# One DMA for a 128-row result tile in place of two of 64 rows, in a kernel of cosine attention and a two-layer product

## The chip, the cores and the metric

One core of a Trainium2 chip runs the whole kernel. The metric is the device time of one execution in microseconds, as the median of several runs. The profile is one more execution, recorded by the hardware profiler. Its span is some microseconds under the device time.

## What is computed

Attention with normalised q and k over 8 batches, 12 heads, 448 positions and 64 channels, then a two-layer product with a hard-swish between the layers, over 3584 tokens:

```python
q_n = q / (norm(q) + 1e-6);  k_n = k / (norm(k) + 1e-6)
attn = softmax(q_n @ k_n.T / tau)
x = (attn @ v)            # 3584 tokens x 768, tokens = batch x position
h = x @ w_in              # 768 -> 2048
g = h * clip(h + 3, 0, 6) / 6
out = g @ w_out           # 2048 -> 768, float32
```

Only the store of `out` is touched here: 3584 rows of 768 float32, 11.0 MB.

## The kernel before

The program is laid out by hand: a plan gives the order of all steps, and each engine runs its own in that order. Heads are treated in pairs, 48 in all. SyncE issues nearly all transfers, on one queue: the loads of q and k (`raw`) and v (`vr`), the transposes by DMA that turn normalised q and k into `tT` and the attention's result into `xT`, and the stores of the result.

```python
def load_qk(j, *heads):            # 448 KB; a load runs two to three pairs ahead of its use
    ...
    nc.sync.dma_start(out=raw_of[j][:, g, :, :].rearrange("p g c d -> p g (c d)"), in_=f[:, g, :])

def load_v(d):                     # four DMAs of 128 KB
    ...
            nc.sync.dma_start(out=o, in_=f[:, :, 3 * half * D : (3 * half + 4) * D])

def crossbar(j):                   # normalised q or k -> tT
    ...
    nc.sync.dma_start_transpose(out=crossed(j)..., in_=nrm...)

def back_crossbar(i):              # attention's result -> xT
    ...
    nc.sync.dma_start_transpose(out=xT[b % 2]..., in_=on...)
```

Positions are read so that partition p of a head holds positions 7p to 7p + 6. Column c (0 to 6) of that grouping gives 64 positions, one in seven. A row tile of the second product holds the 64 positions of one column and then the 64 of another: two columns c and c + 1 of one batch, or, in the fourth tile of a pair of batches, column 6 of the batch before and column 0 of this one.

One unit of the second product is 16 matmuls for 128 rows and 384 columns. The result leaves PSUM through ScalarE and VectorE in turn into `o` (four buffers) and goes to memory from there:

```python
def mm2_unit(b, t, m, end=None):
    ...
    width = MH if end is None else MH // 2          # MH = 384
    cols = slice(m * MH + width * (end or 0), m * MH + width * (end or 0) + width)
    for fc in range(FCN):                           # 16
        ...
        nc.tensor.matmul(ps[:, 0:width], lhs, w_out_sb[:, fc, cols], start=..., stop=...)

    def store():
        o = sb.tile([128, MH], FP32, name="o", tag="o", bufs=4)
        if on_act:
            nc.scalar.copy(out=o[:, 0:width], in_=ps[:, 0:width])
        else:
            nc.vector.tensor_copy(out=o[:, 0:width], in_=ps[:, 0:width])
        unread[key] = 0
        for e in range(2):
            if t < 3:
                r = out[b * S : (b + 1) * S].rearrange("(p c) m -> c p m", c=7)[2 * t + e + b % 2]
            else:
                r = out[(b - 1 + e) * S : (b + e) * S].rearrange("(p c) m -> c p m", c=7)[6 * (1 - e)]
            eng = nc.scalar if end == 1 and e else nc.sync
            eng.dma_start(out=r[:, cols], in_=o[64 * e : 64 * e + 64, 0:width])
```

The very last unit is cut in two of 192 columns, so that its second half is short. There are 55 full units and two half ones: 57 units and 114 stores. A store of 64 rows goes to rows that lie 7 x 768 floats apart, 1536 bytes in each.

Of the kernel before, what the change touches and what calls it, by code (L numbers as in the profile page):

```python
# [61 lines left out]
def kernel(  # L62
# [10 lines left out]
    nc = tc.nc  # L73
    B, H, S, D = q.shape
    d_model, d_ff = moe_w_in.shape
# [194 lines left out]
    def bank_of(name, reads):  # L270

        bank = {"Y": Y, "Z": Z}[name] if name else next_bank()
        key = id(bank)
        assert not unread.get(key), name
        unread[key] = reads
        return bank, key
# [246 lines left out]
    def mm2_unit(b, t, m, end=None):  # L523
        assert not weights
        g = gT[(b // 2) % 2]
        ps, key = bank_of(None, 1)
        width = MH if end is None else MH // 2
        cols = slice(m * MH + width * (end or 0), m * MH + width * (end or 0) + width)
        for fc in range(FCN):
            c0 = (S + SR) * (b % 2) + 128 * t if t < 3 else SM  # L530
            lhs = g[:, fc, c0 : c0 + 128]
            nc.tensor.matmul(  # L532
                ps[:, 0:width],
                lhs,
                w_out_sb[:, fc, cols],
                start=(fc == 0),
                stop=(fc == FCN - 1),
# [6 lines that stand above are left out]
            else:  # L544
                nc.vector.tensor_copy(out=o[:, 0:width], in_=ps[:, 0:width])  # L545
            unread[key] = 0
            for e in range(2):
                if t < 3:
                    r = out[b * S : (b + 1) * S].rearrange("(p c) m -> c p m", c=7)[2 * t + e + b % 2]
                else:  # L550
                    r = out[(b - 1 + e) * S : (b + e) * S].rearrange("(p c) m -> c p m", c=7)[6 * (1 - e)]
                eng = nc.scalar if end == 1 and e else nc.sync
                eng.dma_start(out=r[:, cols], in_=o[64 * e : 64 * e + 64, 0:width])

        evac_n[0] += 1
        on_act = evac_n[0] % 2 == 1
        post["a" if on_act else "v"].append(store)

    def second(b):
# [205 lines left out]
```

## Time and profile before

| | |
|---|---|
| device time, median of 3 runs | 428.23 us (426.42 to 429.01) |
| span of the profiled execution | 422.8 us |
| TensorE busy | 411.1 us, 97% |
| ScalarE, VectorE, GpSimd busy | 64%, 52%, 43% |
| moved by DMA | 65.82 MB, 156 GB/s in the mean |
| stores of the result | 114, of 96 KB (four of 48 KB) |
| first and last store issued | 99.3 and 419.5 us |

How to read the page: its first part has the busy time of each engine; then come the span in 40 slices, the DMA queues with the share of 16 DMA engines that their packets took, the chain of work that ended last (followed back from the last instruction to what released each step), the costliest groups of instructions, and the DMA issues with the time from issue to landing. The letters SPq stand for SyncE's queue, where transfers are issued. A line such as "L553" is a line of the kernel; L553 is the store, L302 the transpose into `tT`, L480 that into `xT`, L174 the load of q and k, and L186 the load of v. In a timeline of SyncE, the first number of a row is when the issue began, the second how long the issuing took, and the last how many in a row.

### The profile page before, as it was taken

The page shows a single profiled execution, that of the slowest core. Times are in us where ns is not written, and L with a number is a line of the kernel's source. Part 1 is how long each engine was busy: PE and PEld are TensorE (multiplying, and loading weights), DVE is VectorE, ACT ScalarE, POOL GpSimd, SP SyncE. Part 2 cuts the span into 40 slices and gives each one's busy share as a digit, 9 for nine tenths or more (in the row PEclk, how much of TensorE's full clock was granted, in tenths as well). Part 3 has the DMA queues.
Part 4 walks back from the last instruction along what each step waited for, and adds up shares of the span by engine and source line. Part 5 has one row for each costly group of instructions (what it writes and reads, how often), then busy time and mean ns, then how long its engine had stood idle before and what let it go on. Part 6 is the DMA issues. An engine that isn't in the chain of part 4 may idle for free.

```text
span 422.8 us, 9251 instructions
## 1 busy us (share of the span) xinstructions
PE 411.1 (97%) x3574; PEld 243.2 (58%) x3575; DVE 217.7 (52%) x419; ACT 271.2 (64%) x593; POOL 181.1 (43%) x184
## 2 busy tenths in 40 slices
PE   6999999999997999999999999999999999999996
PEld 5556655556654555656555555555555555655564
DVE  7689777675443454465455454554554343214410
ACT  6899989977555765866756775676765675105400
POOL 5997787512235456365365464374472200000000
PEclk9999999999999999999999999999999999999999
DMA  8997999996879767676995856668666251330033
GB/s 287 307 244 201 243 194 226 220 194 145 210 170 203 174 175 138 167 194 127 179 193 136 183 156 156 158 154 188 164 160 95 63 75 33 70 75 19 2 75 76
DMA packets 94156, 65.82 MB, mean 156 GB/s; under 512 B 58656, under 2 KB 92576, under 8 KB 94112
## 3 DMA queue, kind: packets, MB, share of 16 engines
q1 hardware_dynamic: 90320, 58.89, 60.4%
q0 software_dynamic: 3712, 6.29, 8.7%
q8 instruction: 28, 0.46, 0.5%
q14 instruction: 16, 0.13, 0.1%
q10 hardware_dynamic: 80, 0.05, 0.0%
HBM read 47.19 MB, written 11.01 MB: 138 GB/s over the span
## 4 chain that ended last, share of the span: by engine, by line
PE 88%; ACT 4%; DMA 4%; SPq 2%; issue 1%; POOL 0%; DVE 0%; ACTq 0%; POOLq 0%
PE M L496 22%; PE M L532 22%; PE PV L433 11%; PE Y L496 6%; PE M L394 6%; PE Z L496 5%; PE Y L532 5%; PE Z L532 5%; ACT at L412 3%; DMA tT<-nrm 2%; PE Z L394 2%; DMA raw<-in_k_dram 1%; PE SC L394 1%; PE Y L394 1%; PE PV L603 1%; DMA vr<-in_v_dram 1%
## 5 line engine op out<-in xcount | busy, mean ns | idle before, releaser
L532 PEld LDWEIGHTS <-gT 128*128 128x128 bf16 x912 | 88.7, 98 | 58.6
L412 ACT ACTIVATE at<-M 128x448 bf16<-128x448 f32 x195 | 94.9, 568 | 30.5 <-PE M L394 25.3
L496 PEld LDWEIGHTS <-w_in_sb 128*128 128x128 bf16 x768 | 74.1, 98 | 67.1 <-issue 3.4
L532 PE MATMUL M<-w_out_sb,gT 128*128 128x384 bf16 (+1 forms) x640 | 106.0, 322 | 0.0
L496 PE MATMUL M<-xT,w_in_sb 128*128 128x448 bf16 x510 | 104.2, 352 | 0.0
L246 POOL TENSOR_TENSOR nrm<-raw,r 128x896 bf16<-128x896 f32 (+1 forms) x45 | 74.2, 1655 | 26.6 <-ACT r L234 22.9
L203 POOL TENSOR_TENSOR sq<-raw 128x896 f32<-128x896 f32 (+3 forms) x42 | 67.8, 1618 | 28.9 <-DMA raw<-in_k_dram 11.6
L511 DVE SCALAR_TENSOR_TENSOR gT<-u,M 128x448 bf16<-128x448 bf16 x85 | 52.5, 621 | 51.0 <-ACT u L505 49.8
L505 ACT ACTIVATE u<-M,half_bias 128x448 bf16<-128x448 f32 x85 | 55.1, 652 | 20.9 <-PE M L496 19.5
L433 PEld LDWEIGHTS <-at 128*128 128x128 bf16 x1344 | 53.3, 98 | 24.9 <-issue 17.7
L433 PE MATMUL PV<-vx,at 128*128 128x65 bf16 (+1 forms) x1344 | 63.9, 198 | 0.0
L215 DVE TENSOR_REDUCE n<-sq 128x14 f32<-128x896 f32 (+1 forms) x50 | 51.9, 1041 | 3.4 <-POOL nrm L246 2.0
L351 POOL COPY km<-tT 64x128 bf16<-64x128 bf16 x34 | 10.6, 312 | 94.1 <-DVE rc L448 33.7
L543 ACT COPY o<-M 128x384 f32<-128x384 f32 (+1 forms) x21 | 9.9, 471 | 40.9 <-PE M L532 40.9
L449 DVE TENSOR_TENSOR on<-PV,rc 128x512 bf16<-128x512 f32 x48 | 33.2, 692 | 3.5 <-DMA xT<-on 1.9
L545 DVE COPY o<-M 128x384 f32<-128x384 f32 (+1 forms) x19 | 10.4, 547 | 47.7 <-PE M L532 47.7
L394 PE MATMUL M<-tT,kz 64*128 64x448 bf16 (+1 forms) x172 | 33.4, 353 | 1.4 <-DMA tT<-nrm 0.5
L412 ACT ACTIVATE at<-Y 128x448 bf16<-128x448 f32 x48 | 27.4, 571 | 10.9 <-PE Z L394 10.9
L412 ACT ACTIVATE at<-Z 128x448 bf16<-128x448 f32 x51 | 29.0, 569 | 3.0 <-PE M L394 2.7
L496 PE MATMUL Y<-xT,w_in_sb 128*128 128x448 bf16 x138 | 29.9, 352 | 0.0
L448 DVE RECIPROCAL rc<-PV 128x8 f32<-128x8 f32 x48 | 9.9, 206 | 38.2 <-PE PV L433 34.9
L496 PE MATMUL Z<-xT,w_in_sb 128*128 128x448 bf16 x120 | 26.1, 352 | 2.0 <-DMA xT<-on 2.0
(78 smaller groups left out, 342.8 us busy)
## 6 DMA issues: line engine op xcount, KB each, us to landing
vr<-in_v_dram SPq DMA_DIRECT2D x96, 128.0 KB, 3.8
raw<-in_k_dram SPq DMA_DIRECT2D x24, 448.0 KB, 4.4
raw<-in_q_dram SPq DMA_DIRECT2D x24, 448.0 KB, 4.3
out_dram<-o SPq DMA_DIRECT2D x110, 96.0 KB, 2.2
w_in_sb<-in_moe_w_in_dram POOLq DMA_DIRECT2D x4, 768.0 KB, 12.1
w_out_sb<-in_moe_w_out_dram POOLq DMA_DIRECT2D x4, 768.0 KB, 11.2
xT<-on SPq DMA_TRANSPOSE x42, 3.8
tT<-nrm SPq DMA_TRANSPOSE x34, 2.9
```

The source lines that it names most:

```text
L203: engines[e].tensor_tensor(out=o, in0=i, in1=i, op=ALU.mult)
L215: nc.vector.tensor_reduce(out=n2s[d % 2][:, j % 2, c], in_=sq[:, :, :, :].rearrange("p g c d -> p (g c) d")[:, c, :], axis=AX.X, op=ALU.add,)
L246: engines[e].tensor_tensor(out=nrm[:, :, g, :].rearrange("p c g d -> p g c d"), in0=raw_of[j][:, g, :, :], in1=rs[d % 2][3][:, j % 2, :] . ...
L351: nc.gpsimd.tensor_copy(out=km[p, :, p], in_=z[p, 3, :, :])
L394: nc.tensor.matmul(o, ks, qt[rows], start=True, stop=True)
L412: nc.scalar.activation(out=o, in_=x, func=AF.Exp, scale=inv_tau)
L433: nc.tensor.matmul(o, at[:, n, q_cols(i // HP, j)], mv, start=(name == "A0" and j % 2 == 0), stop=last, skip_group_check=True,)
L449: nc.vector.tensor_tensor(out=on[:, :, :, :].rearrange("p (b j) h d -> p b (j h) d", b=2), in0=pv4[:, :, :, 0:D], in1=rc[:, :, :].to_broad ...
L496: nc.tensor.matmul(ps[:, 0:S], w_in_sb[:, cc, fc * 128 : (fc + 1) * 128], x[:, cc, 0:S], start=(cc == 0), stop=(cc == CC - 1),)
L505: nc.scalar.activation(out=u[:, :], in_=ps[:, 0:S], func=AF.Relu, bias=half_bias[:, :], scale=1.0 / 6.0)
L511: nc.vector.scalar_tensor_tensor(out=g[:, fc, c0 : c0 + S], in0=u[:, :], scalar=1.0, in1=ps[:, 0:S], op0=ALU.min, op1=ALU.mult,)
L532: nc.tensor.matmul(ps[:, 0:width], lhs, w_out_sb[:, fc, cols], start=(fc == 0), stop=(fc == FCN - 1),)
```

## The change

Each unit's tile is stored by one DMA from all 128 partitions. Its destination is written as a three-dimensional access pattern: 2 columns of the grouping, 64 rows of each, and the 384 (or 192) floats of a row. The distance between the two halves is one row, or, in the fourth tile, the 442 rows from column 6 of one batch to column 0 of the next. The last half store of the last unit goes out on SyncE as well, and no longer on ScalarE. It is meant to halve the number of stores, with their issuing and their waits.

```diff
-            for e in range(2):
-                if t < 3:
-                    r = out[b * S : (b + 1) * S].rearrange("(p c) m -> c p m", c=7)[2 * t + e + b % 2]
-                else:
-                    r = out[(b - 1 + e) * S : (b + e) * S].rearrange("(p c) m -> c p m", c=7)[6 * (1 - e)]
-                eng = nc.scalar if end == 1 and e else nc.sync
-                eng.dma_start(out=r[:, cols], in_=o[64 * e : 64 * e + 64, 0:width])
+            c = 2 * t + b % 2 if t < 3 else 6
+            row = b * S + c if t < 3 else (b - 1) * S + c
+            step = 1 if t < 3 else S - 6
+            r = bass.AP(
+                tensor=out.tensor,
+                offset=out.offset + row * d_model + cols.start,
+                ap=[[step * d_model, 2], [7 * d_model, 64], [1, width]],
+            )
+            nc.sync.dma_start(out=r, in_=o[:, 0:width])
```

## The prediction

> **What bounds the kernel now.** I read the page first: busy times, DMA queues, chain, DMA issues.
>
> ```profile
> span 422.8 us, 9251 instructions
> PE 411.1 (97%) x3574; PEld 243.2 (58%) x3575; DVE 217.7 (52%) x419; ACT 271.2 (64%) x593; POOL 181.1 (43%) x184
> ...
> q1 hardware_dynamic: 90320, 58.89, 60.4%
> ...
> PE 88%; ACT 4%; DMA 4%; SPq 2%; issue 1%; POOL 0%; DVE 0%; ACTq 0%; POOLq 0%
> ...
> out_dram<-o SPq DMA_DIRECT2D x110, 96.0 KB, 2.2
> ...
> xT<-on SPq DMA_TRANSPOSE x42, 3.8
> tT<-nrm SPq DMA_TRANSPOSE x34, 2.9
> ```
>
> TensorE is the bound: 88% of the chain that ended last, 97% busy. A store lands in 2.2 us and nothing on the chain waits for one. But q1, the queue of SyncE, carries everything together: loads of q, k and v, the transposes that feed TensorE (tT, xT), and the stores. Its packets already take 60.4% of all 16 DMA engines' time.
>
> Next, SyncE's timeline from 95 to 140 us, where stores begin, and the chain of waits over the same stretch.
>
> ```profile
> 99.33 3.67 SPq L553 DMA_DIRECT2D out_dram<-o  x4
> 103.10 1.27 SPq L302 DMA_TRANSPOSE tT<-nrm  x1
> ...
> 106.43 1.17 SPq L553 DMA_DIRECT2D out_dram<-o  x2
> 107.66 2.67 SPq L186 DMA_DIRECT2D vr<-in_v_dram  x4
> ...
> 126.46 1.25 SPq L302 DMA_TRANSPOSE tT<-nrm  x1
> 127.80 2.46 SPq L553 DMA_DIRECT2D out_dram<-o  x4
> 130.37 1.27 SPq L302 DMA_TRANSPOSE tT<-nrm  x1
> ```
>
> ```profile
> 109.72 3.11 DMA vr<-in_v_dram
> ...
> 126.46 3.53 DMA tT<-nrm
> ...
> 130.37 4.58 DMA tT<-nrm
> ```
>
> Transposes and v loads stand behind stores in one queue, and here the chain does wait for them. From 135 us on no DMA stands on it. Last, SyncE's timeline of the tail:
>
> ```profile
> 401.34 18.67 SPq L553 DMA_DIRECT2D out_dram<-o  x17
> ```
>
> Seven full units (two DMAs each) and two half ones (one of their DMAs from ScalarE) leave in 18.7 us: one full unit each 2.6 us, TensorE's pace.
>
> [...]
>
> 1. [...] the DMA is split over k engines, [...] Before: 64 partitions against 64 rows, k = 16. After: 128 partitions against a destination whose outermost dimension is 2, so k = 2. [...] The trace before agrees on the first half (the 64 packets of one store pass in 0.59 us, which one or two engines could not do); it holds no DMA with k below 16.
> 2. [...]
> 3. [...] Of the stores' 1536-byte packets, the shortest and about a fifth take 62 to 66 ns, the median 107 ns. [...]
>
> **The change part by part.**
>
> *Removed:* 57 of 114 store issues at 0.58 us (median of L553): 33 us of SyncE's queue time. SyncE's issuing stands for 2% of the chain, chiefly from 102 to 110 us, with three of the removed issues: at most 2 us gained. The evacuating copies wait for one DMA where they waited for two; no compute instruction is added or removed, and TensorE's order stays.
>
> *Changed:* the bytes, 11 MB, stay; their engines do not. At k = 2 each full store is 64 packets of 1536 bytes on engine 0 and 64 on engine 1. At 62 ns (packets of other sizes move in line: 1792 bytes 74 ns, 1024 bytes 46 ns, 256 bytes 18 ns, all medians of the packet records) that is **3.97 us on two engines**, against 4 packets on each of 16 per half-store. At 107 ns it would be 6.8 us.
>
> *Load of engines 0 and 1.* TensorE's stage of two pairs of heads lasts 16.0 us (by the timeline scores start at 223.5, 231.5 and 239.5 us, pair by pair). Issued in it: 2 raw loads of 16 packets for each engine (2 x 16 x 74 ns = 2.4 us), 4 v loads of 8 (1.5 us), 2 xT of 32 (1.2 us), 2 tT of 56 (2.0 us): 7.1 us. From 140 to 330 us the records hold 28 stores, 2.36 in 16 us: 9.4 us. Sum **16.5 us of work in 16.0 us**: these two engines become as full as TensorE, while the other 14 empty. Three stretches follow.
>
> *a. 99 to 135 us, replayed by hand on engine 0.* Two stores issued from 99.3 start about 1.3 us after issue and end at 108.5; two tT and one raw take it to 111.7, the next store to 115.7, the v loads to 117.2. With 0.9 us from last packet to semaphore v lands at 118, where it lands at 112.8: 5 us later. Ahead of the tT issued at 126.46 then lie three stores and 7.9 us of loads and xT: it ends at 138, 8 to 9 us late. Two stores lie between it and the tT of 130.37: that one lands near 147.6 against 134.95. **About 12.5 us lost.**
>
> *b. 135 to 340 us.* Overload 16.5/16.0 is 3%, some 6 us if the queue stays full. Added to it are waits. The tT of the query side is issued at 225.19 and its scores start at 231.54: 6.35 us, of which it uses 2.9. In that stage two stores are issued from 221.85, so 7.9 us of packets precede it, behind what is still queued: it lands about 2 us late. Stages with two such stores come four times (copies to o at 165, 221, 262 and 317 us), so four times 2 us. In the others one store of 4 us fits in the slack. As the overload and these waits partly cover one another, I choose **11 us**.
>
> *c. The tail.* The first store's packets start 1.3 us after 401.34, at 402.6. Then 7 x 3.97 + 2 x 64 x 34 ns (768-byte packets, shortest 34 ns) = 32.1 us on engines 0 and 1 without a gap (four buffers of o keep three stores queued): 434.7, landed at 435.2, against 421.7 before. **13.5 us lost**; TensorE finishes early and waits. The six units from 366 to 380 need 24 us and are through by 393, so they are not carried over.
>
> Sum: 12.5 + 11 + 13.5 = 37 us, less 1 for SyncE: 36 to 37. On the median of 428.2: **465 us**.
>
> **The rivals.**
>
> - *All 16 engines are still used* (the hardware splits on another dimension). [...] its packets fall from 107 towards 62 ns, and half the issues are gone. As stores aren't on the chain and the tail ends in one small store, this is worth 1 to 3 us: 425 to 428. For it: the trace has no DMA with small k. [...] I give it 5%.
> - *Two engines, but hidden.* Deep prefetch (seven raw buffers, two stages ahead) and four o buffers absorb the latency; only the tail shows: 428 + 13.5 = 441. For it: no DMA on the chain after 135 us. Against it: tT has 6 us of slack, and the first stretch has none.
> - *Two engines, at 107 ns a row.* [...] a store takes 6.8 us; the tail alone becomes 8 x 6.8 = 55 us where 19 stood (+36), and engines 0 and 1 have 7.1 + 16.2 = 23.3 us of work in a 16 us stage: over 550. Against it: the last packets of each store, when others have finished, take 62 to 65 ns.
> - *SyncE blocks.* In the built program its DMAs use eight semaphores in turn, and each waits for the DMA eight before. 13 to 14 DMAs in 16 us means that a mean latency over about 9 us makes SyncE the gate, so later transposes start late too. This would add to b, up to 20 us: 485.
>
> **Range and chances.** Middle 465. Low end: b hidden and half of a, 442. High end: SyncE blocking, or packets of 70 ns, 494. Slower by over 2% (above 436.8) needs only k = 2, since the tail alone brings 3%: 0.93. Within 2%: 0.05. Faster: 0.02.
>
> **What the profile after would show.** Right: store issues halve to 57 of 192 KB, with landing times of 6 us upwards in place of 2.2; store packets at about 62 ns; DMA share of the last slices small (2 of 16 engines) while they last; a tail in which TensorE ends some 10 us or more before the last store lands; DMA tT, vr or xT on the chain between 100 and 340 us, and tT landing in over 5 us at the median. The stretch before 97 us unchanged. Wrong: landing near 2 us (k was 16); a packet median near 107 ns; a chain without DMA before 400 us, which would leave the tail alone; or a loss in the middle far over 25 us, which would mean that I missed how late transposes hold up SyncE, GpSimd's copies of tT or the loads behind them.

## The result, and the profile after

| | before | after |
|---|---|---|
| device time, median | 427.78 us (426.42 to 429.01, 4 runs) | **487.4 us** (487.04 to 488.88, 4 runs) |
| ratio | | 1.1401, 95% interval 1.1357 to 1.1445 |
| span of the profiled execution | 422.8 us | 485.3 us |

The change makes the kernel 14% slower, by 59.6 us. First the page of the changed kernel: busy times, granted clock of TensorE in 40 slices, DMA queue, chain, DMA issues.

```profile
span 485.3 us, 9174 instructions
PE 424.6 (87%) x3574; PEld 248.3 (51%) x3575; DVE 218.4 (45%) x419; ACT 272.1 (56%) x593; POOL 181.3 (37%) x184
...
PEclk9999999999597999899999899999999999999995
...
q1 hardware_dynamic: 88690, 58.94, 72.8%
...
PE 45%; DMA 38%; ACT 5%; SPq 4%; DVE 3%; POOL 2%; issue 2%; POOLq 0%; ACTq 0%; DVEq 0%
DMA tT<-nrm 24%; PE M L532 11%; PE M L496 10%; DMA vr<-in_v_dram 5%; PE PV L433 5%; ACT at L412 4%; PE M L394 3%; PE Z L532 3%; PE Y L496 3%; DMA raw<-in_q_dram 3%; PE Z L496 3%; DMA out_dram<-o 2%; PE Y L532 2%; SPq L302 2%; DMA xT<-on 2%
...
out_dram<-o SPq DMA_DIRECT2D x55, 192.0 KB
```

TensorE held 88% of the chain and holds 45%; DMA rises from 4% to 38%, and most of it is the transposes into tT, which the change does not touch. The same bytes take more of q1's packet time (72.8% against 60.4%): the 256-byte packets of the transposes sum to 2742 us against 1317, at the same median of 18 ns, so a few of them last long (1% are over 1.4 us, where before 1% were over 0.07 us). TensorE's busy time grows by 13.5 us though it runs the same 3574 matmuls, and the clock row shows a 5, a 7 and some 8 where it had only nines. The page gives no landing times on this queue, but the semaphore records of the trace do, where a store now has 3 updates and every other DMA 16 as before. Stores land in 7.4 us at the median and 6.3 at least (median 2.2 before), transposes into tT in 7.2 (2.9 before), as was forecast.

**Two engines, from the packet records.** The store's 1536-byte packets move two at a time, each stream with one packet every 61 ns, 65 ns at the median (107 before). The records do not say which engines carry them: "engines 0 and 1" in the prediction stands for the two. A store that follows another takes 3.93 us, one that begins on an idle queue 4.9 to 5.0: its first half has pauses of 0.1 to 0.3 us between packets. Beside other traffic it is up to 5.8.

**Where the time goes.** Both kernels run the same matmuls in the same order, so the start of the n-th matmul in one trace less its start in the other is the lag of TensorE. Between two such points it splits into more idle time and more busy time:

| stretch (us of the kernel before) | predicted | lag grows | idle | slower matmuls |
|---|---|---|---|---|
| start to 93, before any store | 0 | 3.9 | 3.1 | 0.7 |
| a: 93 to 138 | 12.5 | 17.3 | 11.3 | 6.0 |
| b: 138 to 345 | 11 | 27.4 | 20.7 | 6.7 |
| 345 to the last matmuls | 0 | 0.0 | 0.0 | 0.0 |
| c: tail, last store | 13.5 | 13.9 | | |

The first row is no work of the change: no store has been issued there, and the profiles of six other kernels below, which share these matmuls and their order, show -0.4 to 1.8 us in its place. a, b and c sum to 58.6 us, which is the difference of the medians within 1 us.

Stretch b, in SyncE's timeline and, below it, in the chain:

```profile
328.41 0.58 SPq L555 DMA_DIRECT2D out_dram<-o  x1
329.10 2.78 SPq L302 DMA_TRANSPOSE tT<-nrm  x1
```

```profile
165.37 7.60 DMA tT<-nrm
...
329.10 7.56 DMA tT<-nrm
...
336.80 0.35 PE Y L394
```

A transpose issued 0.7 us after a single store takes 7.56 us to land, and the scores (L394) start when it does. In the packet records 20 of the 256-byte packets of the transposes last 1.8 to 3.1 us there; they end at 335.6 us, just after the store's last packet at 335.4. The issue of it takes 2.78 us. All 34 of these issues, before and then after (ns: least, median, most):

```profile
L302 SPq DMA_TRANSPOSE tT<-nrm x34: 1220/1252/2477, 68.3 to 337.6; - x34
```

```profile
L302 SPq DMA_TRANSPOSE tT<-nrm x34: 1221/1921/6126, 70.1 to 384.1; - x34
```

The 20.7 us of idle time in b come apart by what was issued ahead: nine gaps behind a transpose into tT that follows a single store, 8.6 us in sum, and four gaps behind two stores, 12.1 us. Two of these four wait for tT (6.7 us) and two for xT (5.4 us).

The end of stretch a, in the chain and in SyncE's timeline, is two transposes with two stores between them:

```profile
139.57 14.45 DMA tT<-nrm x2
```

```profile
139.57 1.24 SPq L302 DMA_TRANSPOSE tT<-nrm  x1
140.90 1.38 SPq L555 DMA_DIRECT2D out_dram<-o  x2
142.39 5.12 SPq L302 DMA_TRANSPOSE tT<-nrm  x1
```

Last the tail, SyncE's timeline and then the chain:

```profile
416.21 59.77 SPq L555 DMA_DIRECT2D out_dram<-o  x15
```

```profile
459.91 0.49 ACT o L543
460.40 0.02 issue
460.42 11.69 DMA out_dram<-o
...
472.20 0.32 ACT o L543
```

ScalarE's last copy, of 0.32 us, must wait 11.69 us for a store to give back a buffer of o. From 451 us on stores follow each other without a gap, 3.93 us each, while TensorE makes a tile in 2.6 us.

### The profile page after: what moved, and what is told of

It reads as the page before. It is cut to its first block, busy times and chain, and to the rows that moved or that the text cites. A ratio compares the mean times of both kernels' runs of the same rounds, so it can differ in the third digit from the quotient of the medians.

```text
span 485.3 us, 9174 instructions
## 1 busy us (share of the span) xinstructions
PE 424.6 (87%) x3574; PEld 248.3 (51%) x3575; DVE 218.4 (45%) x419; ACT 272.1 (56%) x593; POOL 181.3 (37%) x184
## 3 DMA queue, kind: packets, MB, share of 16 engines
q1 hardware_dynamic: 88690, 58.94, 72.8%
## 4 chain that ended last, share of the span: by engine, by line
PE 45%; DMA 38%; ACT 5%; SPq 4%; DVE 3%; POOL 2%; issue 2%; POOLq 0%; ACTq 0%; DVEq 0%
DMA tT<-nrm 24%; PE M L532 11%; PE M L496 10%; DMA vr<-in_v_dram 5%; PE PV L433 5%; ACT at L412 4%; PE M L394 3%; PE Z L532 3%; PE Y L496 3%; DMA raw<-in_q_dram 3%; PE Z L496 3%; DMA out_dram<-o 2%; PE Y L532 2%; SPq L302 2%; DMA xT<-on 2%
## 5 line engine op out<-in xcount | busy, mean ns | idle before, releaser
L532 PEld LDWEIGHTS <-gT 128*128 128x128 bf16 x912 | 88.8, 98 | 58.6
L496 PEld LDWEIGHTS <-w_in_sb 128*128 128x128 bf16 x768 | 76.1, 100 | 78.4 <-issue 18.0
L496 PE MATMUL M<-xT,w_in_sb 128*128 128x448 bf16 x510 | 108.1, 361 | 2.7 <-DMA xT<-on 2.5
L433 PEld LDWEIGHTS <-at 128*128 128x128 bf16 x1344 | 55.5, 100 | 29.4 <-issue 22.3
L433 PE MATMUL PV<-vx,at 128*128 128x65 bf16 (+1 forms) x1344 | 66.5, 201 | 2.9 <-DVE on L449 2.9
L394 PE MATMUL M<-tT,kz 64*128 64x448 bf16 (+1 forms) x172 | 36.0, 370 | 20.5 <-DMA tT<-nrm 15.1
L412 ACT ACTIVATE at<-Y 128x448 bf16<-128x448 f32 x48 | 27.4, 571 | 11.2 <-PE Z L394 11.2
L496 PE MATMUL Y<-xT,w_in_sb 128*128 128x448 bf16 x138 | 31.0, 361 | 2.8 <-DMA xT<-on 2.8
L394 PEld LDWEIGHTS <-kz 64*128 64x128 bf16 (+1 forms) x296 | 12.8, 95 | 39.4 <-issue 25.6
L545 DVE COPY o<-M 128x384 f32<-128x384 f32 (+1 forms) x19 | 10.4, 546 | 47.7 <-PE M L532 42.4
## 6 DMA issues: line engine op xcount, KB each, us to landing
w_out_sb<-in_moe_w_out_dram POOLq DMA_DIRECT2D x4, 768.0 KB, 12.8
```

The costliest lines, as they stand in the source:

```text
L394: nc.tensor.matmul(o, ks, qt[rows], start=True, stop=True)
L412: nc.scalar.activation(out=o, in_=x, func=AF.Exp, scale=inv_tau)
L433: nc.tensor.matmul(o, at[:, n, q_cols(i // HP, j)], mv, start=(name == "A0" and j % 2 == 0), stop=last, skip_group_check=True,)
L496: nc.tensor.matmul(ps[:, 0:S], w_in_sb[:, cc, fc * 128 : (fc + 1) * 128], x[:, cc, 0:S], start=(cc == 0), stop=(cc == CC - 1),)
```

## The experiments

### Rows that are neighbours, one DMA over 16 engines

If each tile held 128 consecutive tokens, its destination would be a plain matrix of 128 rows. Here the score matmuls read the queries in natural order, which carries this order through to the result.

```diff
-        kt, qt = kz[i % 2], crossed(jq)[:, :, i % 2, :] if jq >= XJ else qT[i % 4]
+        kt = kz[i % 2]
+        if jq >= XJ:
+            qt = crossed(jq)[:, :, i % 2, :].rearrange("p c n -> p n c")
+        else:
+            qt = qT[i % 4].rearrange("p (c n) -> p n c", c=7)
...
-            nc.sync.dma_start(out=r, in_=o[:, 0:width])
+            row = (b - b % 2) * S + c0
+            nc.sync.dma_start(out=out[row : row + 128, cols], in_=o[:, 0:width])
```

> One DMA for each tile of 128 rows as in the change, but the queries are read by the score matmuls in natural order, so that the 128 rows are neighbours in memory and the destination is 128 rows of 1536 bytes, outermost dimension 128. Theory A (two of 16 DMA engines are overloaded): all 16 engines serve a store, the loss is gone: 424 to 428 us, store packets spread over 16 engines, landing near 2 us. Theory B (one DMA of 128 partitions, or its larger size, costs by itself): 470 us or more remain. If TensorE reads the queries slower with the stride, the score matmuls rise from 353 ns and the time with them.

Measured: 531.61 us, ratio 1.2429 (1.2384 to 1.2473). The time is a miss, for the reason named last: the strided read. Groups of instructions, L398 being the score matmul:

```profile
L398 PE MATMUL M<-tT,kz 64*128 64x448 bf16 (+1 forms) x172 | 95.4, 920 | 0.0
```

920 ns in place of 353, so TensorE is busy for 522 us. The stores themselves show what the run was for. From the DMA issues:

```profile
out_dram<-o SPq DMA_DIRECT2D x55, 192.0 KB, 1.8
```

One DMA of 192 KB lands in 1.8 us at the median, less than 96 KB did before (2.2), and DMA has 1% of the chain. A DMA of 128 partitions is not slow by itself. The kernel also serves as the base of a series.

### Fewer engines by the number of rows alone

Same kernel, plain two-dimensional destinations, but each tile in two DMAs, split after 122, 124 or 127 rows:

```diff
-            nc.sync.dma_start(out=out[row : row + 128, cols], in_=o[:, 0:width])
+            for p0, p1 in ((0, 122), (122, 128)):
+                nc.sync.dma_start(out=out[row + p0 : row + p1, cols], in_=o[p0:p1, 0:width])
```

> The kernel with neighbouring rows, but each tile leaves in two DMAs of 122 and 6 rows. [...] the first uses two engines with 61 rows each, with a plain two-dimensional destination. Theory A: as slow as the change, 478 to 495 us. Theory B (the three-dimensional destination is the cost): 425 to 432. Theory C (SyncE's eight semaphores gate it): twice as many stores share them, so clearly slower than the change, over 500.

> As the kernel of 122 rows, with 124 and 4 rows: four engines with 31 rows each, 1.9 us of packets for a store. Theory A: these engines have 7.1 + 2.36 x 1.9 = 11.6 us of work in a stage of 16 us and keep pace with the tail (1.9 against 2.6 us): 428 to 438 us. Theory C: well over 450, as the number of DMAs is that of the kernel of 122 rows.

> As the kernel of 122 rows, with 127 and 1 rows: one engine with 127 rows, 7.8 us of packets for a store. Theory A: 55 x 7.8 + 2 x 4.6 + 107 us of other work after the first store, all on one engine: at least 100 + 545 = 645 us, up to 690. Theory B or C: near the kernel of 122 rows.

| rows of the large DMA | engines, as estimated | device time | against the base |
|---|---|---|---|
| 128 | 16 | 531.61 us | |
| 124 | 4 | 531.86 us | +0.3 |
| 122 | 2 | 555.77 us | +24.2 |
| 127 | 1 | 703.49 us | +171.9 |

The absolute numbers expected for 122 and 124 supposed a base of 428 and are misses; what tells the theories apart is the order. Two rows less of 124 cost 24 us and three rows more cost 172, in the order of the estimated engines: the loss follows neither the bytes nor the number of DMAs. With 124 rows there are as many DMAs as with 122, and nothing is lost: the number of DMAs alone costs nothing here, which speaks against theory C, though this kernel gives SyncE more time in each stage. The loss at two engines is smaller here than in the change, probably because the stage is longer; that was not tried by itself. For 127 the reckoning held: its first store is issued at 134 us, and 134 + 545 = 679 us of one engine's work stand against a span of 701.6.

### A three-dimensional destination over 16 engines

The two halves of the tile are copied side by side to 64 partitions, and the destination has the 64 rows outermost:

```diff
-            o = sb.tile([128, MH], FP32, name="o", tag="o", bufs=4)
+            o = sb.tile([64, 2, MH], FP32, name="o", tag="o", bufs=2)
+            for e in range(2):   # two copies of 64 partitions, ScalarE or VectorE as before
+                ... out=o[:, e, 0:width], in_=ps[64 * e : 64 * e + 64, 0:width]
...
-                ap=[[step * d_model, 2], [7 * d_model, 64], [1, width]],
+                ap=[[7 * d_model, 64], [step * d_model, 2], [1, width]],
```

> One DMA for each tile, and still a three-dimensional destination, but with the 64 rows outermost and the 2 columns of the grouping inside. For that the two halves of the tile are copied from PSUM to the same 64 partitions, side by side, in two copies (o has two buffers, as it takes twice the room in a partition). 64 rows and 64 partitions: theory A says 16 engines and no loss, 425 to 430 us; the 57 additional copies of some 0.5 us lie on ScalarE and VectorE, which have time. Theory B (the three-dimensional form or the size of one DMA costs): 470 us or more.

Measured: 442.05 us, ratio 1.0336 (1.0285 to 1.0387). 45 us of the loss are gone with nothing but the order of two dimensions and the copies it needs; theory B falls. q1 has 89488 packets, 798 more than in the change: 14 more for each of the 57 stores, by the count of 4-byte packets below 16 engines, where the change has 2. The store lands in 2.8 us at the median; its packets, from 64 partitions, take 113 ns at the median (107 before, also from 64). But 425 to 430 was wrong: the second copy is not beside the work. The chain of this kernel:

```profile
349.51 0.55 DVE o L546
350.06 0.01 issue
350.08 0.57 DVE o L546
350.64 0.04 issue
350.69 0.35 PE M L394
```

The next scores wait for the PSUM bank that the copies empty, so each tile pays about half a microsecond more: the lag in stretch b is 13.8 us for 30 tiles, and nothing in a.

### Fewer bytes on the same two engines

The change, with half and with three quarters of each store's columns. The rest of the result is left out; copies and matmuls stay.

```diff
-                ap=[[step * d_model, 2], [7 * d_model, 64], [1, width]],
+                ap=[[step * d_model, 2], [7 * d_model, 64], [1, width // 2]],
-            nc.sync.dma_start(out=r, in_=o[:, 0:width])
+            nc.sync.dma_start(out=r, in_=o[:, 0 : width // 2])
```

> The change with the three-dimensional destination, but each store carries only the first half of its columns: half of the result is left out, and the copies and matmuls stay. A store is 64 packets of 768 bytes on each of two engines, 36 ns each, 2.3 us. Theory A: 7.1 + 2.36 x 2.3 = 12.5 us of work in a 16 us stage, and 2.3 under the tail's 2.6 us: the tail's loss is gone, and of the loss before it at most 10 us are left: 428 to 438 us. If the two-engine DMA costs by its form and not by its bytes, it stays over 470 us.

> The change with three quarters of each store's columns, the rest of the result left out: packets of 1152 bytes, some 49 ns, 3.1 us for a store on two engines. 7.1 + 2.36 x 3.1 = 14.4 us of work in a 16 us stage, and 3.1 against the tail's 2.6 us. If the loss before the tail comes of the overload alone, it is gone here, and the tail adds 8 x 0.5 + 1 = 5: 431 to 436 us. If it comes of transposes that wait behind a single store, whose slack is just used up (1.3 + 3.1 + 1.0 + 0.9 = 6.3 against 6.35 us), part of it stays: 437 to 455 us.

| columns stored | work of the two engines in a 16 us stage, as estimated | tT lands, median | device time | lag in a | in b |
|---|---|---|---|---|---|
| 192 | 12.5 us | 4.5 us | 431.49 us | 3.6 | 0.2 |
| 288 | 14.4 us | 5.8 us | 451.18 us | 12.8 | 4.5 |
| 384 | 16.5 us | 7.2 us | 487.4 us | 17.3 | 27.4 |

The form is that of the change in all three, and the loss follows the bytes, far more than in proportion: stretch b costs next to nothing with 192 columns, 4.5 us with 288, and 27.4 us with 384, where the transposes land later than the 6.35 us of slack that the prediction read. That is waiting, not a cost for each DMA. It is no lasting backlog either: in b of the change, a store that does not directly follow another has its first packet 1.6 us after its issue at the median and 3.0 at most (1.15 at least). What counts is the one store, or the two, just ahead of a transpose. The 451 us fell in the range expected for waiting transposes, but mostly through stretch a, which I had not put apart in that expectation.

### The tail alone, and all but the tail

```diff
+            if b == B - 1:        # in the other kernel: b < B - 1
+                ... one DMA, as after
+            else:
+                ... two DMAs of 64 rows, as before
```

> The change for the stores of the last batch alone (seven full and two half units), the others as before. Theory A with losses that add up: 428 + 14 = 440 to 443 us, TensorE's order and lag as before up to the tail. If the tail's loss came from what earlier stores left in the queue, it would be under 5 us.

> The change for the stores of all batches but the last, whose stores leave in two DMAs of 64 rows as before. Theory A with losses that add up: 487 - 14 = 472 to 475 us.

Measured: 440.94 us (ratio 1.0316, 1.0281 to 1.0350) and 470.69 us (1.0987, 1.0920 to 1.1055). Against the kernel before on the same chips that is 13.5 and 42.4 us; together 55.9 of the 59.6. The losses add up within what the intervals leave open. In the trace of the second, a and b are 17.2 and 27.8 us, as in the change.

### Stores in a queue of their own

```diff
-            nc.sync.dma_start(out=r, in_=o[:, 0:width])
+            nc.scalar.dma_start(out=r, in_=o[:, 0:width])
```

> The change with all 57 stores issued by ScalarE, [...]. If the loss before the tail is waiting of transposes and loads behind stores in SyncE's ring (order), it shrinks to a few us and the tail stays: 440 to 448 us. If it is work that the two engines cannot finish in time (throughput), it stays at 475 to 490. ScalarE's issuing and its waiting for VectorE's copies may add some us; the kernel with neighbouring rows and stores from ScalarE shows how many.

> Neighbouring rows, one DMA over 16 engines, issued by ScalarE: the control for the stores from ScalarE. 426 to 434 us; whatever is over the same kernel with SyncE's issuing is the cost of ScalarE's issuing.

Measured: 467.6 us (1.0904, 1.0815 to 1.0994), and 529.6 us for the control, against 531.61 us when SyncE issues. So ScalarE's issuing costs nothing in the control, where TensorE is slower and ScalarE has more time; in the kernel itself ScalarE's queue, issuing these stores, stands on the chain with 5%. Neither of the two outcomes I named came: the place in SyncE's queue accounts for some 20 us of the loss, and 40 remain. By the trace, idle time of TensorE shrinks from 20.7 to 5.9 us in b and from 11.3 to 7.4 in a; the tail stays, with 14.6 us. What part of the rest is ScalarE's issuing was not taken apart.

These two runs also let one count the engines. ScalarE's queue is q10 on the page, and it holds stores alone. Its packets and megabytes, first in the kernel before, which has a single half store there, then in the change with stores in a queue of their own, then in the control:

```profile
q10 hardware_dynamic: 80, 0.05, 0.0%
```

```profile
q10 hardware_dynamic: 7410, 11.01, 6.7%
```

```profile
q10 hardware_dynamic: 8208, 11.01, 5.7%
```

80 is 64 rows and 16 packets of 4 bytes. 7410 is 57 stores of 128 rows and 2 such packets, 8208 is 57 of 128 and 16. The packets that move at a time agree: up to 16 of the 64 in the half store of the first line, two in the stores of the change. So I read one 4-byte packet for each engine that takes part. With 122, 124 and 127 rows the records hold 8, 8 and 2 for each tile, which fits the estimated engines of its two DMAs, 2 + 6, 4 + 4 and 1 + 1; the sum alone does not tell 122 from 124.

### Natural order through ScalarE

The score matmuls read as before, the stores are those of the first experiment, and the exponential writes its 448 columns in the order 7n + c:

```diff
+                o = o.rearrange("p g (n c) -> p g c n", c=7)
+                x = x.rearrange("p g (c n) -> p g c n", c=7)
             nc.scalar.activation(out=o, in_=x, func=AF.Exp, scale=inv_tau)
```

> The rows brought into natural order in another place: ScalarE's exponentials read PSUM in the old order and write the attention weights with a stride of 7 columns, so that the score matmuls read without a stride again. One DMA of 128 neighbouring rows for a tile, all 16 engines. If ScalarE's 568 ns for 448 columns stay, theory A says 424 to 428 us, that is the kernel before or slightly better, as 57 issues of 0.6 us are gone and nothing waits. If the strided write costs ScalarE more than a quarter, ScalarE (271 us of 423) comes near the bound and the time rises to 440 or more.

Measured: 772.33 us, ratio 1.8068 (1.7976 to 1.8159). It tells nothing of the stores, only that this is no way to the order wanted:

```profile
L418 ACT ACTIVATE at<-M 128x448 bf16<-128x448 f32 x195 | 365.8, 2148 | 11.3 <-PE M L394 10.0 <-PE Y L394 1.2
```

2148 ns where it took 568. None of the versions that used all 16 engines with one DMA beat the kernel before.

## Why the prediction was right, and what in it was mis-sized

The mechanism that was forecast came: two engines, waits of transposes behind stores, and a long tail. The middle of the forecast was 22 us short, and that the time still fell under the upper end is in part luck: 494 had been set for SyncE's blocking or slower packets, and what filled the gap was waits behind single stores and a slower clock. One sign named for being wrong came, a loss in the middle far over 25 us: a and b lost 44.7 us.

- **Two engines (k = 2): right.** It was an estimate when it was made, as the trace before holds no such DMA. Two packets at a time in the records, and two 4-byte packets for each store; the folded tile (16 such packets with 64 outermost, 442.05 us against 487.4) and the series by rows (+0.3, +24.2 and +171.9 us for 124, 122 and 127) show that it is the outermost dimension, and not size, form or number of DMAs, that made the difference here. The counts read from the records are 2 and 16; 4 engines for 124 rows, 2 for 122 and 1 for 127 were my estimates, with which the series agrees.
- **62 ns a packet, 3.97 us a store: right** for stores that follow another (65 ns median, 61 ns apart, 3.93 us), which settles the rival of 107 ns. The median is 65 ns too with 128 partitions over 16 engines, and 113 with 64 partitions; why these differ was not shown. For a store that starts afresh 3.97 is a fifth too short.
- **The tail, 13.5 us: right**, 13.9 in the trace and 13.5 in the kernel with the tail alone.
- **Stretch a, 12.5 us:** idle time 11.3, so the replay was right in its sum; the lag is 17.3 because of the clock, below.
- **Stretch b, 11 us: mis-sized.** 27.4 came. The step that failed is "In the others one store of 4 us fits in the slack". The prediction's own figures left no room for it: 1.3 us to the first packet, 3.97 for the store, 1.0 for the transpose's own packets and 0.9 to the semaphore, less the 0.7 by which the store is issued earlier, are 6.5 us against a slack of 6.35. Measured, such a transpose lands in 7.6 us (the store ahead takes up to 5.8 us beside other traffic); so single stores stall TensorE too, by 8.6 us in sum. The four stages with two stores, reckoned at 8 us, cost 12.1. Idle time is 20.7 us, about twice the term, and the clock adds 6.7. The part for overload, "some 6 us if the queue stays full", did not come in that form: the queue did not stay full.
- **A term that I did not have: 12.7 us of slower matmuls** in a and b. It is neither copying nor waiting; see the last section.
- **SyncE blocks: in part.** Its issues became longer (the 34 transposes into tT 79.0 us in sum against 45.2, though 57 stores fewer are issued), but the series of 124 and 122 rows speaks against the number of DMAs as the gate. Whether the longer issues cost anything beyond the queue they reflect was not taken apart.
- "Removed: at most 2 us gained" can't be seen beside the loss.

## What to carry to other kernels

Before merging two DMAs into one, look at the outermost dimension of both access patterns as the program carries them: here an outermost 2 put the whole transfer on two of 16 engines (7.4 us to landing at the median), where the same bytes with 64 or 128 outermost had all 16 (2.8 and 1.8 us). The mean DMA load before, 60.4% for q1, said nothing of this, and the estimated load of the two engines, 16.5 us in a stage of 16, said too little: reckon how long the merged transfer holds its engines, and set that against the slack of what is issued right behind it. Here the waits grew much faster than the bytes once that slack was used up, and they showed up at other transfers (the transposes), not at the one that was changed.

## What the runs showed that I had not expected

**The clock fell after gaps, and 12.7 us of slower matmuls came on top of the waiting.** In the changed kernel there are five stretches at half the clock (0.5 granted) before the tail, 30.7 us in all, each 3.4, 6.8 or 10.2 us long; 11.7 of the 12.7 us of slower matmuls lie in them. Each begins at a gap of TensorE of 2.8 to 6.0 us, in its second half or within 0.2 us after it; gaps of up to 2.7 us in that trace are followed by none. That is no rule: with the stores in a queue of their own one drop follows a gap of 1.8 us, and in the kernel with neighbouring rows the clock fell three times though TensorE had no gap in the 7 us before. One of the five, by windows (TensorE's busy time and matmuls, then the clock granted, DMA share as a sum of packet times that can pass 1, GB/s), and the first-layer matmul within it and then before, by groups:

```profile
121.00:132.00 11.00, 7.82 (x47) 0.53 1.15 148
```

```profile
L496 PE MATMUL M<-xT,w_in_sb 128*128 128x448 bf16 x8 | 3.2, 581 | 0.0
```

```profile
L496 PE MATMUL M<-xT,w_in_sb 128*128 128x448 bf16 x510 | 104.2, 352 | 0.0
```

581 ns against 352 in the kernel before, which kept its clock up to its last matmul. That the gaps caused the drops was not tried by filling them; it is read from their order in time.

**Two strided accesses within a partition were dear.** A score matmul that reads bf16 columns out of order took 920 ns for 353, and ScalarE's exponential that writes them every 7th column 2148 ns for 568. Both were meant as free ways to reorder rows.
